# Convolution, Fourier mixing and a two-layer network on one core: copies moved to ScalarE, one more buffer for residuals and for normalised rows, two gathers placed earlier

## The chip, the core and the metric

The kernel runs on one core of a Trainium2 chip. The time is that of one launch on the device, in microseconds (us), taken here as the median of three runs. A core has five engines that work side by side, each through its own instructions in order: TensorE (PE in the profile, its weight loads PEld), VectorE (DVE), ScalarE (ACT), GpSimd (POOL) and SyncE (SP), which here only issues transfers. An engine that waits for a result holds back everything behind the waiting instruction in its own list, and nothing else.

## What is computed

```python
# x: (8, 4224, 192) f32; weight: (8, 7); w1: (192, 768); w2: (768, 192)
w = softmax(weight)                      # 7 taps for each of 8 heads of 24 columns
x = causal_conv(x, w)                    # along the sequence, each head its own taps
X = np.fft.fft(x, axis=1)
X = np.fft.fft(X, axis=2)
u = x + np.real(X)
un = (u - mean(u)) / np.sqrt(var(u) + 1e-06)
out = u + np.maximum(un @ w1, 0.0) @ w2
```

## The kernel before

The eight batches go through one program, each in two parts. The **front** of a batch makes its Fourier transform: the convolution in six chunks of three parts (conv_unit: products pc on TensorE at line 387, copied to xa on ScalarE or VectorE, stored to a scratch in DRAM, sc), its reload in another order (load_x, tile xs), a split of each value into two halves of 16 bits (split_x: XH on ScalarE at line 472, XL on VectorE at line 473), and two stages of products with tables (stage_a: pa, yh, yl; stage_b: pb). stage_b is called eight times a batch. Each call writes a tile V in two halves, one by ScalarE (line 524) and one by VectorE (line 525), and then copies the columns with q = 0, 128x96 values, from V to V0 (line 531). V0 collects these columns of all eight calls and is read only by the ninth step of the batch.

The **steps** are the rest: nine a batch, eight of 4 x 128 rows (it = 0 to 7) and one of 128 rows (it = 8). A step consists of
- load_res: the convolved rows xr, read back from sc by one indirect transfer per 128 rows, which GpSimd issues (line 544): four a step, one for it = 8. The tile xr has three buffers.
- prep: the last products pq (line 574), u copied from them by ScalarE in three pieces (line 591), xr added by GpSimd (line 592), mean and variance mv on VectorE (lines 598 and 599), then 1/sqrt: sd on ScalarE (line 610), w and nm on GpSimd (lines 611, 612), y on VectorE (line 613), and five small steps on GpSimd (lines 614 to 618), which refine y and leave nm = -mean * y. Then un = y * u + nm on ScalarE, four pieces (line 628; for steps 0 and 1 of batch 0 on VectorE, line 623), its upper 16-bit half into hl by ScalarE (line 638) and the rest into hl by GpSimd (line 641). The tile un has one buffer.
- transposes: kt from hl by a transposing transfer, which SyncE issues (line 651).
- mlp_hidden, six times: ph = kt @ w1 on TensorE (line 680), hh = max(ph, 0) in 16 bits on ScalarE (line 684), the remainder hlo on VectorE (line 685). ph has two buffers.
- mlp_out, four times: po = hh @ w2 on TensorE (lines 699, 702, 705), added to u on VectorE (line 711), and the store of u (SyncE).

In the main loop the hidden products of step n, the outputs of step n-1, the end of prep of step n+2 with its transposes, the first part of prep of step n+3 and the gathers of step n+4 are written interleaved; the front of later batches is spread over the steps by tables. A scheduler then takes this order as a wish and sets each engine's own list from it, from the tiles that are free and from its estimate of when each operand is there. So a change in buffers or in one operation's engine moves others too.

Ahead of the main loop stands a hand-written start for batch 0: the gathers of steps 0 and 1, stage_b 0 and 1, both steps' prep and transposes at high priority, then, held back until the last remainder of hl of step 1 has been issued (issue_after(lower[0])), the gathers of steps 2 and 3, then the convolution of batch 1.

from_float64 unpacks the 64-bit weights at the start and borrows the tags kt, hl and un for its scratch; the number of buffers given there must agree with the one in prep.

Of the kernel before, what the change touches and what calls it, by code (L numbers as in the profile page):

```python
# [11 lines left out]
F32 = mybir.dt.float32  # L12
I32 = mybir.dt.int32
U32 = mybir.dt.uint32
AF = mybir.ActivationFunctionType
# [4 lines left out]
B, S, D, HID = 8, 4224, 192, 768  # L20
# [105 lines left out]
def kernel(  # L126
# [13 lines left out]
    nc = tc.nc  # L140
    PSUM = bass.MemoryType.PSUM
    cp = ctx.enter_context(tc.tile_pool(name="cp", bufs=1))
    sb = ctx.enter_context(tc.tile_pool(name="sb", bufs=2))
# [79 lines left out]
    def from_float64(dst, raw, rows, n, name):  # L223

        lo_w, hi_w = (raw[:rows, :, i].bitcast(U32) for i in range(2))

        def tmp(i):
            t = sb.tile([128, HID], F32, tag=("kt", "hl", "un")[i], name=f"cv{i}_{name}", bufs=(3, 2, 1)[i])
            return t[:rows, :n]

        bits, aux, rem = tmp(0), tmp(1), tmp(2)
        V = nc.vector
        SL, SR = ALU.logical_shift_left, ALU.logical_shift_right
        bi, ai, ri = bits.bitcast(U32), aux.bitcast(U32), rem.bitcast(U32)

        V.tensor_scalar(ai, hi_w, 30, 30, op0=SR, op1=SL)
        V.tensor_scalar(bi, hi_w, 5, 2, op0=SL, op1=SR)
        V.tensor_tensor(bi, bi, ai, op=ALU.bitwise_or)
        V.scalar_tensor_tensor(bi, lo_w, 29, bi, op0=SR, op1=ALU.bitwise_or)

        V.tensor_scalar(ri, lo_w, 3, 3, op0=SL, op1=SR)
        V.tensor_scalar(ai, bi, 23, 23, op0=SR, op1=SL)
        V.scalar_tensor_tensor(rem, ri, 2.0 ** -52, aux, op0=ALU.mult, op1=ALU.mult)
        V.tensor_tensor(bits, bits, rem, op=ALU.add)

        V.tensor_scalar(ai, hi_w, 1, 21, op0=SL, op1=SR)
        V.scalar_tensor_tensor(dst, ai, 897, bits, op0=ALU.is_ge, op1=ALU.mult)
# [75 lines left out]
    def load_windows(bt, ch, tag="xt", bufs=2):  # L323

        b = bt.b
        n = D if b < NB0 else HP * GRP
        src = xw[b] if b < NB0 else xv[b - NB0]
        xt = sb.tile([WP, WC, D], F32, tag=tag, name=f"xt_{b}_{ch}", bufs=bufs)[:, :, :n]
        with tc.issue_after(turn[0]) if turn[0] else ExitStack():
            nc.sync.dma_start(xt, src[:, ch * WC : (ch + 1) * WC])  # L330
        bt.xt[ch] = xt
# [172 lines left out]
    def stage_b(bt, it):  # L504

        b = bt.b
        V = sb.tile([128, 2, 2 * NM, CG], F16, tag="V", name=f"V_{b}_{it}", bufs=5)
        for h in range(CG // CT):
            pb = ps.tile([128, CT, 2 * NM], F32, tag="f", name=f"pb_{b}_{it}_{h}", bufs=4)
            for i in range(CT):  # L510
                c = it * CG + h * CT + i

                parts = ((0, 2, NM),) if c else ((0, 1, NM), (1, 2, 0))
                for e0, e1, at in parts:
                    for n, (y, l) in enumerate(((bt.yh, 0), (bt.yh, 1), (bt.yl, 0))):
                        nc.tensor.matmul(
                            pb[NJ * e0 : NJ * e1, i],
                            y[:NBD, c, e0:e1].rearrange("p e j -> p (e j)"),
                            R[:, l, at : at + 2 * NM],
                            start=(n == 0), stop=(n == 2),  # L520
                        )
            src = pb.rearrange("p c m -> p m c")
            vh, vl = (V[:, l, :, h * CT : (h + 1) * CT] for l in range(2))
            nc.scalar.activation(vh, src, AF.Copy, scale=ESC)
            nc.vector.scalar_tensor_tensor(
                vl, src, ESC, vh, op0=ALU.mult, op1=ALU.subtract
            )

        if it == 0:
            bt.V0 = sb.tile([128, 2, 6, 64], F16, tag="V0", name=f"V0_{b}")  # L530
        nc.gpsimd.tensor_copy(
            bt.V0.rearrange("p l m c -> p (l m) c")[:, :, it * CG : (it + 1) * CG],
            V.rearrange("p l (m q) c -> p (l m) q c", q=NQ)[:, :, 0],
        )
        bt.V[it] = V


    def load_res(bt, it, g):

        b = bt.b  # L540
        if g == 0:
            bt.xr[it] = sb.tile([128, 4, D], F32, tag="xr", name=f"xr_{b}_{it}", bufs=3)
        col = 0 if it == Q0 else 1 + 4 * it + g
        nc.gpsimd.indirect_dma_start(  # L544
            bt.xr[it][:, g], None, bt.sc[:S],
            bass.IndirectOffsetOnAxis(ap=rows_sb[:, col : col + 1], axis=0),
        )

    def prep(bt, it):
        b = bt.b  # L550
        xr = bt.xr.pop(it)
# [54 lines left out]
        t = sb.tile([128, 4], F32, tag="t", name=f"t_{b}_{it}", bufs=3)[:, :ng]  # L606
# [10 lines left out]
        G_.tensor_tensor(y, y, t, op=ALU.mult)  # L617
        G_.tensor_tensor(nm, nm, y, op=ALU.mult)  # L618
        yield
        un = sb.tile([128, 4, D], F32, tag="un", name=f"un_{b}_{it}", bufs=1)  # L620
        for g in range(ng):
            if b == 0 and it < 2:
                nc.vector.tensor_scalar(
# [11 lines left out]
        hl = sb.tile([128, 3 * ng, 128], F16, tag="hl", name=f"hl_{b}_{it}")  # L635
# [11 lines left out]
    def transposes(bt, it):  # L647
        hl = bt.hl[it]
        n = hl.shape[1]
        kt = sb.tile([128, n, 128], F16, tag="kt", name=f"kt_{bt.b}_{it}", bufs=3)  # L650
        turn[0] = nc.sync.dma_start_transpose(kt, hl.rearrange("p n d -> p (n d)")).ins
        bt.kt[it] = kt.rearrange("p (g i) t -> p i g t", i=3)
# [93 lines left out]
    def call(f, *a):  # L746
        return lambda: f(*a)
# [43 lines left out]
    turn, lower = [None], [None]  # L791
    first = batches[0]
    for ch in range(NCH):
        tag, bufs = (("hlo", 2), ("xt", 2), ("yh", 1), ("yl", 1))[(0, 0, 1, 1, 2, 3)[ch]]
# [39 lines left out]
    def prep_piece(k):  # L834
        bt, it = steps[k]
        if k not in preps:
            preps[k] = prep(bt, it)
        next(preps[k])
# [4 lines left out]
    def gathers(k):  # L843
        bt, it = steps[k]
        return [call(load_res, bt, it, g) for g in range(1 if it == Q0 else 4)]
# [12 lines left out]
    with tc.issue_after(last_load):  # L858
        nc.sync.dma_start(rows_sb, rows)
        for ch in range(4):  # L860
            load_windows(batches[1], ch, *(("xt", 2), ("xs", 2))[ch // 2])
    for f in gathers(0) + gathers(1):
        f()
    stage_b(first, 0)
    stage_b(first, 1)

    for k in range(2):
        with tc.high_priority():
            for f in sums(k) + rest(k):
                f()  # L870
            transposes(first, k)
    with tc.issue_after(lower[0]):
        for f in gathers(2) + gathers(3):
            f()
    for ch in range(4):
        for part in range(3):
            conv_unit(batches[1], ch, part)
        if ch < 2:
            load_windows(batches[1], ch + 4)
    stage_b(first, 2)  # L880
    for f in sums(2):
        f()
    stage_b(first, 3)
    stage_b(first, 4)
    for n in range(len(steps) + 1):
        bt, it = steps[n] if n < len(steps) else (None, 0)
# [93 lines left out]
```

## Time and profile before

| | |
|---|---|
| time, median of 3 runs | 1337.24 us (1334.99, 1337.24, 1337.45) |
| the profiled execution: time, span | 1339.74 us, 1338.0 us |
| granted TensorE clock, mean | 0.96 of full |
| POOL L544, the gathers | 264, 283.0 us, 1072 ns each |
| POOL L531, the copies to V0 | 64, 17.9 us, 281 ns each |
| ACT L628, un | 256 pieces, 120.2 us, 539 ns each |
| steady period of a batch | 155.2 to 155.4 us |

The profile is of one execution. A row of a timeline gives the start, the time taken, the engine, the line, the operation, what it writes and reads, how many neighbours were joined (x), and in brackets how long the engine stood idle just before and what ended that. A group's row gives the sum and the mean of all instructions of a line. A row of windows gives the length of the stretch, each engine's busy time in it, the granted clock and the share of the transfer engines.

### The profile page before, as it was taken

The page shows a single profiled execution, that of the slowest core. Times are in us where ns is not written, and L with a number is a line of the kernel's source. Part 1 is how long each engine was busy: PE and PEld are TensorE (multiplying, and loading weights), DVE is VectorE, ACT ScalarE, POOL GpSimd, SP SyncE. Part 2 cuts the span into 40 slices and gives each one's busy share as a digit, 9 for nine tenths or more (in the row PEclk, how much of TensorE's full clock was granted, in tenths as well). Part 3 has the DMA queues.
Part 4 walks back from the last instruction along what each step waited for, and adds up shares of the span by engine and source line. Part 5 has one row for each costly group of instructions (what it writes and reads, how often), then busy time and mean ns, then how long its engine had stood idle before and what let it go on. Part 6 is the DMA issues. An engine that isn't in the chain of part 4 may idle for free.

```text
span 1338.0 us, 30108 instructions
## 1 busy us (share of the span) xinstructions
PE 1204.8 (90%) x12224; PEld 943.1 (70%) x12224; DVE 745.0 (56%) x1635; ACT 819.0 (61%) x1562; POOL 666.5 (50%) x1052
## 2 busy tenths in 40 slices
PE   4186689998999989998999989999889998999999
PEld 4175458885777767786778857777567876777767
DVE  7763365456545565456644575446654566555443
ACT  4643387558755686557865586556755667545642
POOL 0236535457445664457444574456634576456520
PEclk9588889998999999999999999999899999999999
DMA  8934395556555566456554576555564444223321
GB/s 274 241 90 125 90 246 142 104 132 166 132 124 128 126 149 144 121 129 167 120 139 103 122 178 127 128 125 129 141 137 108 116 96 95 69 63 84 75 63 39
DMA packets 225819, 170.19 MB, mean 127 GB/s; under 512 B 119560, under 2 KB 207440, under 8 KB 225680
## 3 DMA queue, kind: packets, MB, share of 16 engines
q1 hardware_dynamic: 163408, 108.53, 35.4%
q10 hardware_dynamic: 49600, 33.77, 10.0%
q0 software_dynamic: 12672, 25.97, 7.5%
q8 instruction: 95, 1.56, 0.5%
q14 instruction: 44, 0.36, 0.1%
HBM read 83.73 MB, written 58.55 MB: 106 GB/s over the span
## 4 chain that ended last, share of the span: by engine, by line
PE 35%; POOL 24%; issue 17%; ACT 11%; DVE 5%; DMA 4%; another core or an unknown queue 1%; SPq 1%; ACTq 0%; POOLq 0%; DVEq 0%
PE ph L680 12%; POOL xr L544 11%; PE pa L490 5%; ACT un L628 4%; POOL u L592 4%; PE po L699 4%; PE po L705 4%; PE po L702 4%; POOL hl L641 4%; DMA xs<-sc 3%; PE pc L387 3%; DVE XL L473 2%; PE pq L574 2%; ACT hl L638 2%; ACT hh L684 1%
## 5 line engine op out<-in xcount | busy, mean ns | idle before, releaser
L680 PE MATMUL ph<-kt,W 128*128 128x512 f16 (+1 forms) x2160 | 504.0, 367 | 18.5 <-DMA kt<-hl 8.4
L685 DVE SCALAR_TENSOR_TENSOR hlo<-ph,hh 128x512 f16<-128x512 f32 (+1 forms) x400 | 270.8, 679 | 346.5 <-ACT hh L684 342.0
L699 PE MATMUL po<-W,hh 128*128 128x192 f16 x1584 | 387.9, 248 | 45.7 <-ACT hh L684 34.1
L702 PE MATMUL po<-W,hh 128*128 128x192 f16 x1584 | 387.9, 248 | 1.3 <-issue 1.3
L705 PE MATMUL po<-W,hlo 128*128 128x192 f16 x1584 | 384.1, 247 | 1.8 <-issue 1.5
L684 ACT ACTIVATE hh<-ph 128x512 f16<-128x512 f32 (+1 forms) x400 | 236.5, 593 | 199.2 <-PE ph L680 141.3
L544 POOL DMA_INDIRECT xr<-sc,rows_sb x264 | 283.0, 1072 | 134.4 <-issue 60.7
L680 PEld LDWEIGHTS <-W 128*128 128x128 f16 x2160 | 196.4, 99 | 170.7 <-issue 25.7
L641 POOL TENSOR_TENSOR hl<-un,hl 128x512 f16<-128x512 f32 (+1 forms) x144 | 129.4, 920 | 219.0 <-ACT hl L638 210.4
L699 PEld LDWEIGHTS <-hh 128*128 128x128 f16 x1584 | 155.8, 98 | 58.9 <-ACT hh L684 38.6
L592 POOL TENSOR_TENSOR u<-u,xr 128x768 f32<-128x768 f32 (+1 forms) x72 | 121.1, 1682 | 129.9 <-ACT u L591 129.7
L702 PEld LDWEIGHTS <-hh 128*128 128x128 f16 x1584 | 155.8, 98 | 28.7 <-issue 14.1
L705 PEld LDWEIGHTS <-hlo 128*128 128x128 f16 x1584 | 155.6, 98 | 27.5 <-issue 5.8
L628 ACT ACTIVATE un<-u,nm,y 128x192 f32<-128x192 f32 x256 | 120.2, 539 | 53.9 <-POOL nm L618 49.5
L387 PE MATMUL pc<-xt,band 128*120 128x144 f32 x756 | 120.5, 301 | 24.2 <-DMA band<-line_d 15.0
L387 PEld LDWEIGHTS pc<-xt,band 128*120 128x120 f32 x756 | 107.3, 193 | 32.6 <-issue 16.1
L490 PE MATMUL pa<-c_sb,XH 128*128 128x128 f16 x1024 | 103.2, 223 | 22.2 <-ACT XH L472 19.1
L711 DVE SCALAR_TENSOR_TENSOR u<-po,fo,u 128x384 f32<-128x384 f32 (+1 forms) x136 | 81.4, 599 | 62.1 <-PE po L705 46.7
L473 DVE SCALAR_TENSOR_TENSOR XL<-xs,s_x,XH 128x768 f16<-128x768 f32 x64 | 104.2, 1638 | 17.1 <-ACT XH L472 10.3
L499 DVE SCALAR_TENSOR_TENSOR yl<-pa,yh 99x512 f16<-99x512 f32 x128 | 85.3, 682 | 49.1 <-ACT yh L498 45.7
L472 ACT ACTIVATE XH<-xs,s_x 128x768 f16<-128x768 f32 x64 | 106.3, 1694 | 7.9 <-DMA xs<-sc 7.9
L490 PEld LDWEIGHTS <-XH 128*128 128x128 f16 x1024 | 82.6, 99 | 32.6 <-ACT XH L472 19.7
(125 smaller groups left out, 1461.5 us busy)
## 6 DMA issues: line engine op xcount, KB each, us to landing
out_dram<-u SPq DMA_DIRECT2D x64, 384.0 KB
xt<-in_xw_dram SPq DMA_DIRECT2D x42, 576.0 KB
sc<-xa ACTq DMA_DIRECT2D x42, 540.0 KB
xs<-sc SPq DMA_DIRECT2D x96, 192.0 KB
xs<-sc SPq DMA_DIRECT2D x32, 216.0 KB
xr<-sc,rows_sb POOLq DMA_INDIRECT x264
sc<-xa ACTq DMA_DIRECT2D x7, 450.0 KB
xt<-in_xv_dram SPq DMA_DIRECT2D x6, 504.0 KB
```

The source lines that it names most:

```text
L387: nc.tensor.matmul(pc[:WR, h - h0], band[:, h, :WR], xt[:, :, h * GRP : (h + 1) * GRP], start=True, stop=True,)
L490: nc.tensor.matmul(pa[:, i], x[:, at], F[:, l], start=(n == 0), stop=(n == 2))
L544: nc.gpsimd.indirect_dma_start(bt.xr[it][:, g], None, bt.sc[:S], bass.IndirectOffsetOnAxis(ap=rows_sb[:, col : col + 1], axis=0),)
L592: nc.gpsimd.tensor_tensor(u[:, :ng], u[:, :ng], xr[:, :ng], op=ALU.add)
L628: nc.scalar.activation(un[:, g], u[:, g], AF.Identity, bias=nm[:, g : g + 1], scale=y[:, g : g + 1],)
L641: lower[0] = nc.gpsimd.tensor_tensor(bl[:, :, o : o + n], un[:, :ng, f], hi[:, :, f], op=ALU.subtract).ins
L680: nc.tensor.matmul(ph[:, n], W1[:, w, ht * 128 : (ht + 1) * 128], kt[:, k], start=(i == 0), stop=(i == len(order) - 1),)
L684: anchor[0] = nc.scalar.activation(hh, ph, AF.Relu).ins
L685: nc.vector.scalar_tensor_tensor(hlo, ph, 0.0, hh, op0=ALU.max, op1=ALU.subtract)
L699: nc.tensor.matmul(po[:, g % 2], hh[:, ht, tk], W2[:, ht, 0], start=(ht == 0), stop=False)
L702: nc.tensor.matmul(po[:, g % 2], hh[:, ht, tk], W2[:, ht, 1], start=False, stop=False)
L705: nc.tensor.matmul(po[:, g % 2], hlo[:, ht, tk], W2[:, ht, 0], start=False, stop=(ht == 5),)
```

## The change

Three edits. The copies to V0 run on ScalarE as an activation with AF.Copy. The tile xr has four buffers, and the gathers of steps 2 and 3 stand with those of steps 0 and 1, no longer held back. The tile un has two buffers.

```diff
--- before
+++ after
         def tmp(i):
-            t = sb.tile([128, HID], F32, tag=("kt", "hl", "un")[i], name=f"cv{i}_{name}", bufs=(3, 2, 1)[i])
+            t = sb.tile([128, HID], F32, tag=("kt", "hl", "un")[i], name=f"cv{i}_{name}", bufs=(3, 2, 2)[i])
...
-        nc.gpsimd.tensor_copy(
+        nc.scalar.activation(
             bt.V0.rearrange("p l m c -> p (l m) c")[:, :, it * CG : (it + 1) * CG],
             V.rearrange("p l (m q) c -> p (l m) q c", q=NQ)[:, :, 0],
+            AF.Copy,
         )
...
-            bt.xr[it] = sb.tile([128, 4, D], F32, tag="xr", name=f"xr_{b}_{it}", bufs=3)
+            bt.xr[it] = sb.tile([128, 4, D], F32, tag="xr", name=f"xr_{b}_{it}", bufs=4)
...
-        un = sb.tile([128, 4, D], F32, tag="un", name=f"un_{b}_{it}", bufs=1)
+        un = sb.tile([128, 4, D], F32, tag="un", name=f"un_{b}_{it}", bufs=2)
...
-    for f in gathers(0) + gathers(1):
+    for f in gathers(0) + gathers(1) + gathers(2) + gathers(3):
         f()
...
-    with tc.issue_after(lower[0]):
-        for f in gathers(2) + gathers(3):
-            f()
```

The lines from 532 on stand one lower in the changed kernel, so that the gathers are L545 there, un L629, hh L685. In the lists below a tile's name ends with the step within its batch and a serial number: u_3_1193 is u of step 3; in hh_1_3662<-ph_1_1_3736 the hidden values of step 1 are made from the second of its six products.

GpSimd at the start of batch 0, before: from the addition of step 2 to its normalisation.

```order
L531 COPY V_0_692<-V_6_1133 128x12x8
L592 TENSOR_TENSOR u_2_967<-u_2_967,xr_2_844 128x768
L592 TENSOR_TENSOR u_3_1193<-u_3_1193,xr_3_849 128x768
L544 DMA xr_5_1391<-sc_126,rows_sb 128x192 x4
L544 DMA xr_6_1616<-sc_126,rows_sb 128x192 x4
L531 COPY V_0_692<-V_7_1355 128x12x8
L611 TENSOR_SCALAR w_2_1003<-mv_2_991 128x4
L612 TENSOR_SCALAR nm_2_1004<-mv_2_991 128x4
L592 TENSOR_TENSOR u_4_1404<-u_4_1404,xr_4_1177 128x768
L614 TENSOR_TENSOR t_2_1002<-y_2_1001 128x4
L611 TENSOR_SCALAR w_3_1299<-mv_3_1260 128x4
```

The same engine there after the change:

```order
L593 TENSOR_TENSOR u_2_967<-u_2_967,xr_2_658 128x768
L545 DMA xr_6_1616<-sc_126,rows_sb 128x192 x4
L642 TENSOR_TENSOR hl_0_789<-un_0_784,hl_0_789 128x4x128
L642 TENSOR_TENSOR hl_0_789<-un_0_784,hl_0_789 128x4x64
L642 TENSOR_TENSOR hl_1_848<-un_1_843,hl_1_848 128x4x128
L642 TENSOR_TENSOR hl_1_848<-un_1_843,hl_1_848 128x4x64
L612 TENSOR_SCALAR w_2_1003<-mv_2_991 128x4
L613 TENSOR_SCALAR nm_2_1004<-mv_2_991 128x4
L615 TENSOR_TENSOR t_2_1002<-y_2_1001 128x4
L616 TENSOR_TENSOR t_2_1002<-t_2_1002,w_2_1003 128x4
L617 TENSOR_SCALAR t_2_1002<-t_2_1002 128x4
L618 TENSOR_TENSOR y_2_1001<-y_2_1001,t_2_1002 128x4
```

Before, the gathers of steps 5 and 6 and a copy to V0 stood between step 2's u and its chain (w, nm, t); now the gather of step 6 and the hl of steps 0 and 1 stand there. The gathers of steps 4 and 5 stand further ahead, behind u of step 1.

GpSimd in batch 1, steps 3 and 4 (each later batch reads alike), before:

```order
L592 TENSOR_TENSOR u_4_3745<-u_4_3745,xr_4_3524 128x768
L531 COPY V_1_2540<-V_7_3696 128x12x8
L611 TENSOR_SCALAR w_3_3648<-mv_3_3612 128x4
L612 TENSOR_SCALAR nm_3_3649<-mv_3_3612 128x4
L614 TENSOR_TENSOR t_3_3647<-y_3_3646 128x4
L544 DMA xr_7_4252<-sc_854,rows_sb 128x192 x4
L615 TENSOR_TENSOR t_3_3647<-t_3_3647,w_3_3648 128x4
L611 TENSOR_SCALAR w_4_3900<-mv_4_3808 128x4
L612 TENSOR_SCALAR nm_4_3901<-mv_4_3808 128x4
L614 TENSOR_TENSOR t_4_3899<-y_4_3898 128x4
L616 TENSOR_SCALAR t_3_3647<-t_3_3647 128x4
```

After:

```order
L593 TENSOR_TENSOR u_4_3745<-u_4_3745,xr_4_3524 128x768
L612 TENSOR_SCALAR w_3_3648<-mv_3_3612 128x4
L613 TENSOR_SCALAR nm_3_3649<-mv_3_3612 128x4
L615 TENSOR_TENSOR t_3_3647<-y_3_3646 128x4
L545 DMA xr_8_4568<-sc_854,rows_sb 128x192
L616 TENSOR_TENSOR t_3_3647<-t_3_3647,w_3_3648 128x4
L612 TENSOR_SCALAR w_4_3900<-mv_4_3808 128x4
L613 TENSOR_SCALAR nm_4_3901<-mv_4_3808 128x4
L617 TENSOR_SCALAR t_3_3647<-t_3_3647 128x4
L618 TENSOR_TENSOR y_3_3646<-y_3_3646,t_3_3647 128x4
L619 TENSOR_TENSOR nm_3_3649<-nm_3_3649,y_3_3646 128x4
```

Behind the first small step of t of step 3 stood the four gathers of step 7; now one gather stands there, that of step 8, and those of step 7 are ahead of u of step 4. The copy to V0 is gone.

ScalarE at the same steps, before:

```order
L610 ACTIVATE sd_4_3897<-mv_4_3808,eps 128x4
L684 ACTIVATE hh_1_3662<-ph_1_1_3736 128x512
L472 ACTIVATE XH<-xs_1_3405,s_x_3160 128x64x12
L684 ACTIVATE hh_1_3662<-ph_1_2_3797 128x512
L472 ACTIVATE XH<-xs_2_3636,s_x_3160 128x64x12 x2
L628 ACTIVATE un_3_3672<-u_3_3567,nm_3_3649,y_3_3646 128x192 x4
L684 ACTIVATE hh_1_3662<-ph_1_3_3835 128x512
L343 ACTIVATE sq_0_3845,nrm_3844<-xt_0_3450 128x1152
L638 ACTIVATE hl_3_3728<-un_3_3672 128x4x192
L684 ACTIVATE hh_1_3662<-ph_1_4_3883 128x512
L591 ACTIVATE u_5_3974<-pq_5_3973,g_1276 128x2x192
L591 ACTIVATE u_5_3974<-pq_5_3973,g_1276 128x2x64
```

After:

```order
L611 ACTIVATE sd_4_3897<-mv_4_3808,eps 128x4
L629 ACTIVATE un_3_3672<-u_3_3567,nm_3_3649,y_3_3646 128x192 x4
L685 ACTIVATE hh_1_3662<-ph_1_1_3736 128x512
L472 ACTIVATE XH<-xs_1_3405,s_x_3160 128x64x12
L639 ACTIVATE hl_3_3728<-un_3_3672 128x4x192
L629 ACTIVATE un_4_3931<-u_4_3745,nm_4_3901,y_4_3898 128x192 x4
L685 ACTIVATE hh_1_3662<-ph_1_2_3797 128x512
L472 ACTIVATE XH<-xs_2_3636,s_x_3160 128x64x12 x2
L639 ACTIVATE hl_4_3957<-un_4_3931 128x4x192
L685 ACTIVATE hh_1_3662<-ph_1_3_3835 128x512
L343 ACTIVATE sq_0_3845,nrm_3844<-xt_0_3450 128x1152
L685 ACTIVATE hh_1_3662<-ph_1_4_3883 128x512
```

un of step 3 moved from behind three XH to the place behind sd of step 4, ahead of the hh of step 1, and un and hl of step 4 moved ahead of its hh as well.

## The prediction

> **What bounds the kernel now.** I read the page's busy shares first, then the table of windows over one batch, then the waits of the engine that is busiest.
>
> ```profile
> PE 1204.8 (90%) x12224; PEld 943.1 (70%) x12224; DVE 745.0 (56%) x1635; ACT 819.0 (61%) x1562; POOL 666.5 (50%) x1052
> L699 PE MATMUL po<-W,hh 128*128 128x192 f16 x1584 | 387.9, 248 | 45.7 <-ACT hh L684 34.1
> L628 ACT ACTIVATE un<-u,nm,y 128x192 f32<-128x192 f32 x256 | 120.2, 539 | 53.9 <-POOL nm L618 49.5
> core 0: us, PE busy (x) PEld busy (x) DVE busy (x) ACT busy (x) POOL busy (x), PEclk, DMA share, GB/s
> 100.00:255.50 155.50, 126.85 (x1219) 97.93 (x1217) 75.63 (x160) 90.00 (x168) 74.96 (x119) 0.90 0.64 147
> 410.92:566.13 155.21, 147.94 (x1532) 116.05 (x1531) 86.24 (x189) 102.64 (x197) 84.44 (x132) 0.99 0.58 134
> ```
>
> TensorE sets the time: 90% over the span, and 147.94 of 155.21 us (95%) in a middle batch, with 7.3 us of gaps. The first batch's stretch is looser: 126.85 of 155.5, so 28.7 us idle. A change that gives TensorE no less work can win only in those two places. Its largest named wait after the start is for hh from ScalarE (34.1 us over the run), and ScalarE itself waits 49.5 us at un for nm from GpSimd. The rows of TensorE's timeline where the start and a middle batch lose most:
>
> ```profile
> 105.01 2.32 PE L680 MATMUL ph<-kt,W 128*128 128x512 f16 x10 [0.30 <-DMA kt<-hl]
> 123.32 0.34 PE L699 MATMUL po<-W,hh 128*128 128x192 f16 x1 [7.15 <-ACT hh L684]
> 166.89 4.33 PE L680 MATMUL ph<-kt,W 128*128 128x512 f16 x10 [8.09 <-DMA kt<-hl]
> 176.93 3.39 PE L387 MATMUL pc<-xt,band 128*120 128x144 f32 x16 [4.13 <-DMA xt<-in_xw_dram]
> 190.69 1.24 PE L680 MATMUL ph<-kt,W 128*128 128x512 f16 x5 [1.08 <-DVE hlo L685]
> 478.87 0.24 PE L699 MATMUL po<-W,hh 128*128 128x192 f16 x1 [1.71 <-DVE u L711]
> 482.05 0.34 PE L699 MATMUL po<-W,hh 128*128 128x192 f16 x1 [2.28 <-ACT hh L684]
> ```
>
> 105.01 is the first hidden product of step 0, 166.89 that of step 2 (step 1's stands between). The last two rows are the two larger gaps of batch 2.
>
> **The start: why step 2 comes late, and what the change does to it.** GpSimd's timeline:
>
> ```profile
> 68.40 0.95 POOL L544 DMA_INDIRECT xr<-sc,rows_sb  x1 [0.31 <-issue]
> 81.23 0.26 POOL L531 COPY V<-V 128x96 f16<-128x96 f16 x1 [11.88 <-DVE V L525]
> 83.64 3.61 POOL L592 TENSOR_TENSOR u<-u,xr 128x768 f32<-128x768 f32 x2 [1.17 <-ACT u L591]
> 98.72 1.78 POOL L641 TENSOR_TENSOR hl<-un,hl 128x512 f16<-128x512 f32 x2 [2.73 <-ACT hl L638]
> 104.84 1.08 POOL L544 DMA_INDIRECT xr<-sc,rows_sb  x1
> 118.90 0.95 POOL L544 DMA_INDIRECT xr<-sc,rows_sb  x1 [0.31 <-issue]
> 123.68 1.81 POOL L592 TENSOR_TENSOR u<-u,xr 128x768 f32<-128x768 f32 x1
> 131.20 0.99 POOL L544 DMA_INDIRECT xr<-sc,rows_sb  x1
> 140.01 0.95 POOL L544 DMA_INDIRECT xr<-sc,rows_sb  x1 [0.30 <-issue]
> 143.97 0.26 POOL L531 COPY V<-V 128x96 f16<-128x96 f16 x1 [3.02 <-DVE V L525]
> 158.27 0.35 POOL L618 TENSOR_TENSOR nm<-nm,y 128x4 f32<-128x4 f32 x2
> 161.31 1.78 POOL L641 TENSOR_TENSOR hl<-un,hl 128x512 f16<-128x512 f32 x2 [2.27 <-ACT hl L638]
> 103.10 1.22 ACT L591 ACTIVATE u<-pq,g 128x384 f32<-128x384 f32 x3 [0.29 <-PE pq L574]
> ```
>
> Step 2's u is ready on ScalarE at 104.3, but GpSimd adds its residual only at 123.68, since twelve gathers stand ahead (104.84 to 119.85, so 1.25 each), and normalises it at 158.3, since eight more gathers, a V copy that waits 3.02 and the gathers of step 7 stand ahead again. Afterwards the gathers of steps 2 and 3 are issued behind those of steps 0 and 1, in GpSimd's idle 69.35 to 81.23 (8 x 1.25 = 10.0 fits the 11.9), and no V copy is left there. By the new order, with these durations: u of 0 and 1 end at 87.25; the gathers of 4 and 5 (8 x 1.25) at 97.3; fourteen small steps of about 0.25 us at 100.8; u of step 2 waits for ScalarE until 104.3 and ends at 106.1; the gather of 6 (4 x 1.25) at 111.1; hl of step 0 at 112.9, of step 1 at 114.7; the chain, un, hl of step 2 at about 121. From hl's end to ph took 166.89 - 163.09 = 3.8 us, so **step 0's ph stands at about 117 instead of 105, step 2's input at 125 instead of 166.9**.
>
> Terms, for TensorE. (a) The wait of 8.09 goes: +8.1. (b) Behind it ten products took 4.33 us, where five later took 1.24 (248 each): 1.85 lost there, gone with the wait: +1.9. (c) xt at 176.93 is issued on SyncE behind step 2's transpose, which no longer holds the queue; but TensorE's new order also asks for it some 25 us sooner. It lands after the loads of batch 1 whose stores end in the 130s either way. From 0 to 4.1 gained; I take 2. (d) Step 0 is 12 us later. About one and a half steps of stage B are drawn ahead of it, and TensorE idled in that stretch anyway (7.15 at 123.32, with small waits for issue before it). If the 7.15 is the same idleness, the delay costs about 2; if it comes back as well, 9. I take 2. **Sum 8.1 + 1.9 + 2 - 2 = 10 us gained**; bounds 3 (7.15 comes back) and 17 (all of xt, no loss at step 0, 3 us of issue waits).
>
> [...]
>
> **The middle batches: what moves on GpSimd and ScalarE.** Times of batch 2, steps 3 and 4:
>
> ```profile
> 469.33 0.19 POOL L614 TENSOR_TENSOR t<-y 128x4 f32<-128x4 f32 x1
> 469.68 1.08 POOL L544 DMA_INDIRECT xr<-sc,rows_sb  x1 [0.16 <-POOL t L614]
> 476.31 0.56 POOL L615 TENSOR_TENSOR t<-t,w 128x4 f32<-128x4 f32 x1
> 476.95 1.35 POOL L611 TENSOR_SCALAR w<-mv 128x4 f32<-128x4 f32 x1
> 479.58 0.19 POOL L617 TENSOR_TENSOR y<-y,t 128x4 f32<-128x4 f32 x1
> 470.36 0.28 ACT L610 ACTIVATE sd<-mv,eps 128x4 f32<-128x4 f32 x1
> 479.66 1.86 ACT L628 ACTIVATE un<-u,nm,y 128x192 f32<-128x192 f32 x4 [3.46 <-POOL nm L618]
> 483.05 0.83 ACT L638 ACTIVATE hl<-un 128x768 f16<-128x768 f32 x1
> 485.33 0.60 ACT L684 ACTIVATE hh<-ph 128x512 f16<-128x512 f32 x1
> 470.50 1.56 DVE L473 SCALAR_TENSOR_TENSOR XL<-xs,s_x,XH 128x768 f16<-128x768 f32 x1
> L531 POOL COPY V<-V 128x96 f16<-128x96 f16 x64 | 17.9, 281 | 94.6 <-DVE V L525 94.5
> L524 ACT ACTIVATE V<-pb 128x408 f16<-128x408 f32 x128 | 63.6, 514 | 63.8 <-PE pb L516 23.9 <-remote 20.2 <-PE ph L680 18.2
> L213 ACT ACTIVATE r_x<-r_x 128x1 f32<-128x1 f32 x8 | 1.6, 203 | 18.2 <-DVE r_x L212 16.8 <-issue 1.4
> ```
>
> Between t and its successor stood four gathers (469.68 to 476.3); one stands there now. So nm of step 3 is ready after 469.7 + one gather (1.25) + six small steps (0.2 each): about 472.2, and about 473.5 if VectorE's XL, which runs from 470.50, stretches them as it stretched w at 476.95 (1.35 us). But un of step 3 also moves: from behind three XH to directly behind sd (ends 470.64), so it now waits W = 1.5 to 2.9 us there, with five hh of step 1 queued behind it. Between 470.64 and the end of hh at 485.9 ScalarE had the 3.46 of waiting; now it has W, and un and hl of step 4 (1.86 + 0.83 = 2.7) that stood behind. The last hh of step 1 moves by W + 2.7 - 3.46 = W - 0.8, so +0.7 to +2.1 us. TensorE waits there for hh already (2.28 at 482.05), so some of it is on the path; its own order puts products of step 0 ahead meanwhile. Bounds per batch: -0.8 (W = 0) and +2.1; I take +0.7, the smaller end, as part of it is covered. It occurs in six batches: **+4 us**, bounds -5 and +13.
>
> [...]
>
> **The 64 copies on ScalarE.** No such copy stands in the trace on ScalarE. Bounds: 203 ns (L213, one column) and 514 ns (L524, 408 columns); on GpSimd it took 281. It has 96 columns, so nearer to the lower row: I take 0.3, or 19 us of busy time in all (13 to 33). ScalarE is busy 102.64 of 155.21, so 8 x 0.3 = 2.4 per batch fit; it hurts only where one stands ahead of an hh that TensorE waits for. Each also waits for VectorE's half of V, on GpSimd 94.5/64 = 1.5 us each, now with hh behind. I take 1 us on the path in all; bounds 0 and 13 (a seventh of the wait per batch, or all 33 us at 40% exposure). [...]
>
> **The second un buffer** takes away a wait that ScalarE hardly has (un waits for nm, 49.5 of 53.9); it costs nothing by itself, and its effect is the new place of un, priced above. **The fourth xr buffer** moves the same 264 gathers earlier; 0 outside the start.
>
> **Sum.** -10 + 4 + 1 = -5 us from the profiled execution's 1339.74, so 1334.7. The median of the three runs is 1337.24, 2.5 lower, so the forecast is **1332.2 us** as a median. Measured against no change, about 0.2% (2.7 us) can be told.
>
> **The rivals.** *More is won* (0.2): the early nm does on ScalarE what the 49.5 us of waiting promises, and of TensorE's 34.1 - 7.15 = 27 us of waiting for hh half goes: -10 - 13 = -23, so 1314. For it: the gathers leave the middle of every chain. Against: un now waits at the front of ScalarE's queue. *ScalarE's queue* (0.25, the other side): un waits W = 2.9 with hh of step 1 behind it in six batches, +13, and the copies cost 5 rather than 1: -10 + 13 + 5 = +8, so 1345. It decides from the point where a batch loses 1.5 us (six times that eats nine of the ten won). For it: XL's stretch; against: TensorE's cover. *The start does not shorten* (0.15): step 0 at 117 costs all its 9, xt is waited for, so 3 won: -3 + 4 + 1 = +2, so 1339; the early gathers would only have exchanged which step is late. *Forecast* (0.4): 1326 to 1338.
>
> **Range.** From 1314 to 1346: the lower end is the larger gain, the upper that of ScalarE's queue; outside is left a start that both fails and pays. Faster by over 0.2% (below 1334.5): all of the first rival, 0.65 of the forecast's 0.4, 0.02 of the others: 0.48. Within 0.2%: 0.12 of the forecast's, 0.08 of the unshortened start's: 0.2. Slower: 0.32.
>
> **What would show it.** Right at the start: TensorE's first ph of step 0 near 117, that of step 2 near 150 without a wait for kt, and the stretch 100 to 255 busier than 126.85. In the middle: batch periods of 155.2 to 157.5, un of step 3 with a wait of 1.5 to 2.9 at sd. The copy: 0.27 to 0.35 us in ScalarE's group of line 531. I would be wrong if periods fall below 154 (un no longer blocks hh), or if step 2's ph still comes after 160.

## The result and the profile after

The changed kernel takes 1353.53 us (median of four runs, 1352.34 to 1355.44) where the kernel before, timed beside it, takes 1337.35: a ratio of 1.0124, with a 95% interval of 1.0108 to 1.0140. It is slower by 16 us. The forecast was 1332.2. The times and ratios below are of fast runs; the one slow run, of the kernel with the fourth xr buffer (1884.21 us at a granted clock of 0.612), is left out.

The changed kernel's page, the busy times and the rows that answer to those of before (lines stand one lower from 532 on):

```profile
PE 1208.6 (89%) x12224; PEld 941.0 (70%) x12224; DVE 747.0 (55%) x1635; ACT 830.7 (61%) x1626; POOL 644.2 (48%) x988
L700 PE MATMUL po<-W,hh 128*128 128x192 f16 x1584 | 386.9, 248 | 46.7 <-ACT hh L685 41.3
L629 ACT ACTIVATE un<-u,nm,y 128x192 f32<-128x192 f32 x256 | 119.9, 537 | 72.9 <-POOL nm L619 72.5
L531 ACT ACTIVATE V<-V 128x96 f16<-128x96 f16 x64 | 17.9, 280 | 18.3 <-DVE V L525 18.2
```

TensorE does the same work (1208.6 against 1204.8) in a longer span. Its wait for hh rose from 34.1 to 41.3 us although the 7.1 us of the start's largest one went out of it, and ScalarE's wait at un for nm rose from 49.5 to 72.5. The copies took what they took on GpSimd, 280 ns.

Where the 16 us arise is seen by laying both traces side by side at one instruction, the first hh of a step:

| first hh of | before, us | after, us | difference |
|---|---|---|---|
| batch 0, step 0 | 106.3 | 133.6 | +27.3 |
| batch 0, step 2 | 169.5 | 173.6 | +4.0 |
| batch 0, step 3 | 192.0 | 191.8 | -0.2 |
| batch 1, step 1 | 312.9 | 312.6 | -0.3 |
| batch 2, step 1 | 468.3 | 471.7 | +3.3 |
| batch 4, step 1 | 779.0 | 787.6 | +8.6 |
| batch 6, step 1 | 1094.4 | 1107.2 | +12.8 |
| batch 7, step 7 | 1316.7 | 1332.2 | +15.5 |

So the start came out even, where 10 us were forecast as won, and each middle batch loses about 3 us, in its steps 1 to 3: from the first hh of step 1 to that of step 4 it takes 59.9 us instead of 56.7 (mean of batches 1 to 4). Two things have to be explained.

**The start.** TensorE's timeline of the changed kernel, the waits from the first stage A to the first ph of step 0:

```profile
68.03 0.28 PE L490 MATMUL pa<-c_sb,XH 128*128 128x128 f16 x2 [0.79 <-issue]
75.04 0.27 PE L490 MATMUL pa<-c_sb,XL 128*128 128x128 f16 x1 [1.13 <-issue]
81.46 0.26 PE L490 MATMUL pa<-c_sb,XH 128*128 128x128 f16 x1 [1.16 <-issue]
105.16 1.81 PE L387 MATMUL pc<-xt,band 128*120 128x144 f32 x10 [3.11 <-issue]
131.22 4.42 PE L681 MATMUL ph<-kt,W 128*128 128x512 f16 x10 [8.76 <-DMA kt<-hl]
```

The products of stage A, which before ran back to back, come one or two at a time from 71.6 on, with gaps that no operand explains (13 waits of pa for issue, 9.2 us in all, against one of 0.3 in the kernel before). They lie where the gathers of steps 2 and 3 now run. The table of windows shows the same stretch, 69 to 81 us, first in the kernel before:

```profile
69.00:81.00 12.00, 10.59 (x184) 9.79 (x181) 9.88 (x16) 8.86 (x17) 0.35 (x1) 1.00 0.05 13
```

and in the changed kernel:

```profile
69.00:81.00 12.00, 4.14 (x31) 2.29 (x31) 2.21 (x4) 1.57 (x3) 7.61 (x9) 0.63 0.28 74
```

The columns are TensorE, its weight loads, VectorE, ScalarE, GpSimd, the granted clock, the share of the transfer engines, GB/s. 31 products are issued instead of 184, while the transfer engines are 28% busy, and VectorE and ScalarE stand idle most of the time too. The first V of batch 0 comes at 90.9 instead of 79.6 us.

**The middle.** ScalarE's timeline of the changed kernel in batch 2, steps 3 and 4, and under it GpSimd's, with one row of VectorE's, and TensorE's:

```profile
473.71 0.30 ACT L611 ACTIVATE sd<-mv,eps 128x4 f32<-128x4 f32 x1
477.08 1.86 ACT L629 ACTIVATE un<-u,nm,y 128x192 f32<-128x192 f32 x4 [3.07 <-POOL nm L619]
478.85 0.57 ACT L685 ACTIVATE hh<-ph 128x512 f16<-128x512 f32 x1
481.57 1.85 ACT L629 ACTIVATE un<-u,nm,y 128x192 f32<-128x192 f32 x4
490.66 1.21 ACT L592 ACTIVATE u<-pq,g 128x384 f32<-128x384 f32 x3 [0.89 <-DMA out_dram<-u]
491.75 0.60 ACT L685 ACTIVATE hh<-ph 128x512 f16<-128x512 f32 x1
```

```profile
473.15 1.06 POOL L545 DMA_INDIRECT xr<-sc,rows_sb  x1 [0.16 <-POOL t L615]
474.24 1.48 POOL L616 TENSOR_TENSOR t<-t,w 128x4 f32<-128x4 f32 x1
474.17 1.54 DVE L473 SCALAR_TENSOR_TENSOR XL<-xs,s_x,XH 128x768 f16<-128x768 f32 x1
476.85 0.20 POOL L619 TENSOR_TENSOR nm<-nm,y 128x4 f32<-128x4 f32 x1
```

```profile
479.48 0.26 PE L700 MATMUL po<-W,hh 128*128 128x192 f16 x1 [2.12 <-ACT hh L685]
483.10 0.24 PE L700 MATMUL po<-W,hh 128*128 128x192 f16 x1 [1.41 <-DVE u L712]
488.20 0.34 PE L700 MATMUL po<-W,hh 128*128 128x192 f16 x1 [1.27 <-ACT hh L685]
```

un of step 3 waits 3.07 us directly behind sd, five hh of step 1 stand behind it, and un of step 4 behind the first of these. One gather stands in nm's chain instead of four, yet the first small step behind it took 1.48 us where such a step takes 0.2, beside VectorE's XL of 1.54. In batches 1, 3, 4 and 5 the same step, at 315.17, 632.36, 790.13 and 948.64, took 1.47 or 1.48, each time beside an XL. TensorE waits for hh at 479.48 and 488.20. The last line of the first fence is the sixth hh of step 1, 20.1 us behind the first (471.65); in the kernel before that distance is 17.0.

### The profile page after: what moved, and what is told of

Its sections match the earlier page's. It is cut to its first block, busy times and chain, and to the rows that moved or that the text cites. A ratio compares the mean times of both kernels' runs of the same rounds, so it can differ in the third digit from the quotient of the medians.

```text
span 1353.5 us, 30076 instructions
## 1 busy us (share of the span) xinstructions
PE 1208.6 (89%) x12224; PEld 941.0 (70%) x12224; DVE 747.0 (55%) x1635; ACT 830.7 (61%) x1626; POOL 644.2 (48%) x988
## 4 chain that ended last, share of the span: by engine, by line
PE 44%; POOL 15%; ACT 12%; issue 12%; DVE 9%; DMA 5%; SPq 1%; POOLq 0%; ACTq 0%; another core or an unknown queue 0%; DVEq 0%
PE ph L681 17%; POOL xr L545 7%; PE po L700 5%; PE po L706 5%; PE po L703 5%; PE pa L490 5%; ACT un L629 4%; DVE XL L473 4%; PE pc L387 3%; POOL u L593 3%; PE pq L575 3%; DMA out_dram<-u 3%; ACT XH L472 2%; POOL hl L642 2%; DVE hlo L686 2%
## 5 line engine op out<-in xcount | busy, mean ns | idle before, releaser
L700 PE MATMUL po<-W,hh 128*128 128x192 f16 x1584 | 386.9, 248 | 46.7 <-ACT hh L685 41.3
L685 ACT ACTIVATE hh<-ph 128x512 f16<-128x512 f32 (+1 forms) x400 | 235.0, 589 | 197.1 <-PE ph L681 149.6
L545 POOL DMA_INDIRECT xr<-sc,rows_sb x264 | 280.3, 1062 | 134.7 <-issue 60.7
L629 ACT ACTIVATE un<-u,nm,y 128x192 f32<-128x192 f32 x256 | 119.9, 537 | 72.9 <-POOL nm L619 72.5
L387 PE MATMUL pc<-xt,band 128*120 128x144 f32 x756 | 116.6, 296 | 20.1 <-DMA band<-line_d 15.0
L490 PE MATMUL pa<-c_sb,XH 128*128 128x128 f16 x1024 | 106.0, 225 | 25.3 <-ACT XH L472 18.4
L387 PEld LDWEIGHTS pc<-xt,band 128*120 128x120 f32 x756 | 104.2, 189 | 28.9 <-issue 18.3
L498 ACT ACTIVATE yh<-pa 99x512 f16<-99x512 f32 x128 | 74.6, 598 | 62.0 <-PE pa L490 24.9
L472 ACT ACTIVATE XH<-xs,s_x 128x768 f16<-128x768 f32 x64 | 105.8, 1684 | 10.4 <-DMA xs<-sc 6.7
## 6 DMA issues: line engine op xcount, KB each, us to landing
xs<-sc SPq DMA_DIRECT2D x96, 192.0 KB
```

The costliest lines, as they stand in the source:

```text
L387: nc.tensor.matmul(pc[:WR, h - h0], band[:, h, :WR], xt[:, :, h * GRP : (h + 1) * GRP], start=True, stop=True,)
L490: nc.tensor.matmul(pa[:, i], x[:, at], F[:, l], start=(n == 0), stop=(n == 2))
L545: nc.gpsimd.indirect_dma_start(bt.xr[it][:, g], None, bt.sc[:S], bass.IndirectOffsetOnAxis(ap=rows_sb[:, col : col + 1], axis=0),)
L629: nc.scalar.activation(un[:, g], u[:, g], AF.Identity, bias=nm[:, g : g + 1], scale=y[:, g : g + 1],)
L685: anchor[0] = nc.scalar.activation(hh, ph, AF.Relu).ins
L700: nc.tensor.matmul(po[:, g % 2], hh[:, ht, tk], W2[:, ht, 0], start=(ht == 0), stop=False)
```

## The experiments

The runs were spread over several chips, and the kernel before takes 1336 to 1338 us on some of them and 1314 on two. Each ratio is to the kernel before on the same chip. "Period" is a quarter of the time from the first hh of step 1 in batch 1 to that in batch 5; "six hh" the time from the first to the sixth hh of step 1 in batch 2; W the wait of un of step 3 there.

| run | ratio (95%) | period | six hh | W | first V |
|---|---|---|---|---|---|
| before, again | 1 (single run) | 155.1 | 17.0 | 3.46 | 79.4 |
| changed kernel, again | 1.0116 (1.0101 to 1.0132) | 158.6 | 20.1 | 3.08 | 92.2 |
| without the second un buffer | 1.0095 (1.0078 to 1.0112) | 157.9 | 18.0 | 3.06 | 91.3 |
| without the copies on ScalarE | 1.0011 (0.9997 to 1.0026) | 156.2 | 17.9 | 1.92 | 89.3 |
| un late, all three edits | 0.9847 (0.9834 to 0.9861) | 152.9 | 15.6 | 0 | 92.7 |
| gathers held, all three edits | single run, 1357.5 us | 158.6 | 20.2 | 3.08 | 79.0 |
| un late, copies, new start | 0.9791 (0.9778 to 0.9805) | 153.5 | 15.5 | 0 | 79.3 |
| *chips with 1314:* copies alone | 0.9992 (0.9978 to 1.0006) | 153.4 | 17.6 | 3.98 | 79.1 |
| second un buffer alone | 1.0138 (1.0120 to 1.0157) | 155.7 | 19.5 | 3.46 | 80.4 |
| fourth xr buffer alone | 1.0053 (1.0039 to 1.0066) | 154.9 | 18.1 | 1.91 | 81.1 |
| fourth xr buffer, early gathers | 1.0013 (1.0001 to 1.0025) | 155.3 | 18.1 | 1.91 | 79.7 |
| before, un late | 0.9807 (0.9789 to 0.9824) | 150.3 | 15.3 | 0 | 78.8 |

### One edit at a time

The copies alone:

```diff
-        nc.gpsimd.tensor_copy(
+        nc.scalar.activation(
...
+            AF.Copy,
```

> The copies to V0 on ScalarE alone; xr keeps three buffers, un one, the gathers of steps 2 and 3 stay held back. In this kernel un of step 3 stays behind the three XH on ScalarE. Theory A (the middle batches lose because un of steps 3 and 4 stands ahead of the hh of step 1 on ScalarE): nothing moves, 1335 to 1340 us, batch period 155.2 to 155.6. Theory B (the 64 copies themselves hold ScalarE up): the 16 us are here, 1350 or more, period about 157.9.

Ratio 0.9992: nothing. Theory B, that the copies by themselves hold ScalarE up, falls; ScalarE's list keeps un where it was.

The second un buffer alone:

```diff
-        un = sb.tile([128, 4, D], F32, tag="un", name=f"un_{b}_{it}", bufs=1)
+        un = sb.tile([128, 4, D], F32, tag="un", name=f"un_{b}_{it}", bufs=2)
```

> The second un buffer alone. On ScalarE un of step 4 now stands directly behind un of step 3, and un and hl of step 4 (2.7 us) ahead of the last hh of step 1. Theory A: the last hh of step 1 comes up to 2.7 us later, so period 156.5 to 158 and 1345 to 1354 us. Theory B: 1337, period 155.2.

Ratio 1.0138: on this chip one line loses as much as the whole change did. ScalarE's timeline of this kernel in batch 2:

```profile
467.54 3.61 ACT L628 ACTIVATE un<-u,nm,y 128x192 f32<-128x192 f32 x8 [3.46 <-POOL nm L618]
471.05 0.57 ACT L684 ACTIVATE hh<-ph 128x512 f16<-128x512 f32 x1
473.89 0.83 ACT L638 ACTIVATE hl<-un 128x768 f16<-128x768 f32 x1
```

Eight pieces of un in one go, steps 3 and 4 together, with the hh behind them, and step 4's hl among them. The sixth hh comes 19.5 us behind the first, 1.9 later than in the copies alone on the same chip (17.6); 2.7 was worked out from un and hl of step 4. With one buffer, un of step 4 could not start before the hl of step 3 had read the buffer; that had kept it out of the way.

The fourth xr buffer alone, and with the early gathers:

```diff
-            bt.xr[it] = sb.tile([128, 4, D], F32, tag="xr", name=f"xr_{b}_{it}", bufs=3)
+            bt.xr[it] = sb.tile([128, 4, D], F32, tag="xr", name=f"xr_{b}_{it}", bufs=4)
```

> The fourth xr buffer alone, gathers of steps 2 and 3 still held back. On ScalarE un of step 3 stands behind one hh and one XH of step 1 rather than directly behind sd, un of step 4 ahead of the last hh, its hl behind it. Theory A: the last hh moves by 1.86 plus the wait of un for nm minus 3.46; with a wait of 1 to 3 that is -0.6 to +1.4 a batch, so 1333 to 1346. Theory B: 1337. The start gains only from the order behind the held gathers, 0 to 5 us.

> Fourth xr buffer and the early gathers, copies on GpSimd, un with one buffer. The middle as in the run with the fourth buffer alone. The start tells whether the sixteen gathers in a row slow TensorE: theory C (gaps of issue in the first stage A come with the gathers that run beside it): the first V of batch 0 at 90 to 92 us as in the changed kernel, instead of 80. Rival D (the gaps have to do with the copies on ScalarE or the un buffer): the first V at 80 to 81.

1.0053 and 1.0013. The periods (154.9, 155.3) lie 1.5 and 1.9 above the 153.4 of the copies alone, which stand for the kernel before on that chip. The sum W + 1.86 - 3.46 gives +0.3 for the hh, and they moved by 0.6 against the copies alone; so the rest of the 1.5 is lost elsewhere, and the sum doesn't cover it. The early gathers give back some 5 us at the start (1320.8 to 1315.8). And on this chip stage A is not disturbed, with the same sixteen gathers in a row:

```profile
69.00:81.00 12.00, 10.37 (x184) 9.77 (x183) 9.79 (x16) 9.42 (x19) 8.36 (x9) 1.00 0.30 83
```

The gaps of theory C stay out, as rival D expected. But the kernel lacks the copies and the un buffer and the chip is another too, and the next runs speak for the chip.

### The whole change again, and without one edit

> The changed kernel as it is, on the chip on which the single edits were timed. Theory A (un and hl of step 4 ahead of the last hh of step 1 cost a middle batch 2.5 us): the middle loses 15 us against before. Theory C (sixteen gathers in a row starve TensorE's issue): first V of batch 0 near 91 us as in the first profile; if that is a matter of the chip or the moment (rival D2), it stands near 80 here and the start gains 5 to 10, so that the ratio is 1.004 to 1.010 rather than 1.012.

> The kernel before as it is, for its profile on this chip. Without the gaps of issue behind the gathers of steps 2 to 4 (theory D2) the first hh of step 2 comes near 152 us instead of 169.5; with them it is near 169 again.

These two ran on another chip than the single edits, one of those with 1337. The first V is at 92.2 and the gaps are back; the ratio is that of the first measurement. The kernel before loses time in the same manner where its own twelve gathers run (104.84 to 119.85): its wait of 7.15 at 123 in the prediction's rows is 8.70 here, and its step 2 has its first hh at 169.2. On the chips with 1314 it comes at 152 to 158 in the kernels that keep the start. The stretch of these twelve gathers as windows, first in the first profile of the kernel before, then in the copies alone on a chip with 1314:

```profile
104.00:124.00 20.00, 9.32 (x89) 5.70 (x87) 5.20 (x9) 5.46 (x12) 13.51 (x19) 0.81 0.49 141
104.00:124.00 20.00, 20.00 (x204) 15.51 (x202) 13.31 (x41) 12.03 (x26) 16.16 (x16) 1.00 0.68 193
```

That speaks for D2, that this belongs to the chip, and so do the two runs that follow on it: each leaves out one of the edits, and the gaps are there all the same (first V at 91.3 and 89.3). No kernel with the early gathers ran on both kinds of chip. The ratio that D2 expected was for a chip without the gaps.

> Copies on ScalarE, fourth xr buffer, early gathers; un with one buffer. On ScalarE un of step 3 stands directly behind sd of step 4 as in the whole change, three of the four pieces of un of step 4 ahead of the hh of the fourth product, the last piece and hl ahead of the last hh. Theory A: the middle loses 1.5 to 2.5 us a batch, ratio 1.007 to 1.012. Theory E (it is the second un buffer by itself): nothing, ratio 1.000 to 1.002.

> Second un buffer, fourth xr buffer, early gathers; the copies stay on GpSimd. On ScalarE un of steps 3 and 4 stand together behind one hh and one XH of step 1, ahead of its last four hh. Theory A: 1.5 to 2.5 us a batch, ratio 1.007 to 1.012. Theory F (the early nm lets un start sooner and pays for it): 0 to 1 us a batch, ratio 1.000 to 1.005.

Without the second un buffer the ratio is 1.0095: theory A's range, and E falls. Here un of step 3 stands directly behind sd again, with the wait of 3.06; the six hh lose only 1.0 of the 2.8 us of the period. 1.6 more are lost within step 2 (from its first hh to that of step 3 19.3 us instead of 17.6), where TensorE waits 1.00 for XL at 493.71. Without the copies on ScalarE, the other two edits kept, the ratio is 1.0011: un of step 3 then stands behind one hh and one XH, W is 1.9, and a batch loses 1.1. By the ratio that is F's range, not A's. So the cheap copies matter, though not by their time; the lists show how: with them and the fourth xr buffer un goes up directly behind sd.

### The place of un alone

All three edits stay; the end of prep is asked for behind the fourth product of the step rather than behind the first, and un is held behind the hh just written:

```diff
-                nc.scalar.activation(
-                    un[:, g], u[:, g], AF.Identity,
+                with in_turn():
+                    nc.scalar.activation(
+                        un[:, g], u[:, g], AF.Identity,
...
-            place(rest(n + 2), 0, 1)
-            place([call(transposes, *steps[n + 2])], 3, 1)
+            place(rest(n + 2), 6, 1)
+            place([call(transposes, *steps[n + 2])], 8, 1)
```

> All three edits as in the changed kernel; only un moves: the end of prep is asked for four products later, and un is held on ScalarE behind the hh of the product just written, so that un of step 3 stands behind the fourth hh of step 1 (as in the kernel before), with nm long ready, and no un of step 4 stands among the hh of step 1. Theory A (the middle batches lose by the place of un and its wait): the middle loses nothing or wins, from hh of the first to hh of the sixth product of step 1 at most 17 us instead of 20.1, period 153 to 155.3, ratio to the kernel before 0.985 to 1.002. Rival G (three edits take the time elsewhere, by buffers, copies or transfers): period stays near 158, ratio 1.010 or more.

Ratio 0.9847, where the same three edits without it give 1.0124, and the disturbed start is kept (first V at 92.7). ScalarE's timeline in batch 2, the fourth hh of step 1 and un of step 3:

```profile
471.13 0.57 ACT L686 ACTIVATE hh<-ph 128x512 f16<-128x512 f32 x1
471.61 1.85 ACT L630 ACTIVATE un<-u,nm,y 128x192 f32<-128x192 f32 x4
473.37 1.61 ACT L472 ACTIVATE XH<-xs,s_x 128x768 f16<-128x768 f32 x1
```

un waits for nothing any more, and one un stands among the hh of a step. TensorE's waits in this kernel:

```profile
PE po L701 <- ACT hh L686: 10.2, 13, 1.6
```

41.3 us became 10.2. From the first hh of step 1 to that of step 4 a batch takes 56.6 us again (56.7 before, 59.9 in the changed kernel): what the middle had lost is back. Another 2.2 us a batch are won around step 0: from its first hh to that of step 1 16.0 us instead of 20.8, less 2.6 lost in the steps from 4 on. Rival G falls: the buffers, copies and transfers are all still there. And the last version below, on the same chip and without the two buffers, has a period of 153.5 beside 152.9 here, so once un is late the buffers cost the middle nothing.

The same in the kernel before, with nothing else changed:

> The kernel before with nothing but un placed late, as in the run of the whole change with un late; copies on GpSimd, three xr buffers, one un buffer, start as before. Theory A: the middle wins as there, period 153 to 154, 8 to 14 us in all, ratio 0.988 to 0.995, and the three edits add nothing to that in the middle. If the gain there needed the early nm, which the fourth xr buffer brings: 0.997 to 1.003.

Ratio 0.9807, below the expected range: the gain was there to be had without any of the three edits, and it doesn't need the early nm. It isn't won in step 1, as theory A would have it: from the first hh of step 1 to that of step 4 a batch takes 57.0 us, and 56.1 in the copies alone on such a chip. It is won from the first hh of step 0 to that of step 1, 16.2 us instead of 20.7. There un of step 2 now stands behind the sixth hh instead of behind the first, and products pc of a convolution have left that stretch as well; what each is worth is not separated.

### The gathers at the start

The changed kernel with the gathers of steps 2 and 3 behind u of step 1:

```diff
-    for f in gathers(0) + gathers(1) + gathers(2) + gathers(3):
+    for f in gathers(0) + gathers(1):
         f()
...
+    with tc.issue_after(adds[1]):
+        for f in gathers(2) + gathers(3):
+            f()
```

> The changed kernel, but the gathers of steps 2 and 3 held on GpSimd behind the addition of step 1's residual, thus behind the first stage A. Theory C (gathers in a row slow TensorE's issue, where the chip shows it at all): the first V of batch 0 at 80 us, no gaps of issue in stage A; the gaps come with the gathers, now between 87 and 112 us. Rival: the gaps stay in stage A at 68 to 82 us whatever GpSimd does, first V near 91. Middle as in the changed kernel, period 158.

Windows of this kernel, stage A and then the stretch of the gathers:

```profile
69.00:81.00 12.00, 10.45 (x180) 9.69 (x180) 10.01 (x18) 8.86 (x17) 0.00 (x0) 1.00 0.04 11
88.00:108.00 20.00, 5.78 (x46) 4.88 (x44) 4.94 (x17) 0.81 (x2) 15.48 (x21) 0.65 0.61 184
```

TensorE's largest gap in it:

```profile
104.37 0.33 PE L516 MATMUL pb<-c_sb,yh 99*128 99x102 f16 x2 [8.34 <-issue]
```

Stage A is whole, the first V at 79.0, and the gaps moved with the gathers: 46 products in 20 us, another stage and other operands. On this chip a row of gathers slows what TensorE issues. The end is much the same as with the early gathers (1357.5 in a single run; the changed kernel's runs lie between 1350 and 1357), since the gaps only changed place.

A version from this: the kernel before with the copies on ScalarE, un late, and at the start step 4's gathers behind step 2's u and those of steps 5 and 6 behind the normalisation of steps 2 and 3.

```diff
+        after = None
+        if b == 0 and it > 3:
+            after = adds.get(2) if it == 4 else nms.get(it - 3)
+        with tc.issue_after(after) if after is not None else ExitStack():
```

> The kernel before with the copies on ScalarE, un placed late as in the run before, and at the start the gathers of step 4 behind the addition of step 2, those of steps 5 and 6 behind the normalisation of steps 2 and 3; three xr buffers, one un buffer. Theory A: period 153 to 155, so 0 to 13 us won in the middle; at the start step 2's input comes 10 to 25 us sooner where the gathers slowed TensorE, 0 to 10 us won. Ratio 0.982 to 0.998. If neither counts: 1.000.

Ratio 0.9791, below both kernels, and below 0.982, where the range ended. Step 2's first hh comes at 145.7 instead of 169.2. How much of the gain is the start's is not separated: un late in the kernel before gave 0.9807 on a chip without the gaps, and the two intervals overlap.

## Why the prediction was wrong

The sum was -10 for the start, +4 for the middle, +1 for the copies. Measured: 0, about +16, 0.

- **Start, the step that failed:** "in GpSimd's idle 69.35 to 81.23 (8 x 1.25 = 10.0 fits the 11.9)". They did fit, from 69.35 to 79.05, but that GpSimd was idle did not make them free: TensorE's stage A was stretched, and the first V came 11.4 us later. The delays behind were followed rightly: ph of step 0 was put at 117 and came at 131.2, which is 117 and 11, with 3 more because u of step 2 left ScalarE at 118.3, 14 behind the 104.3 used. The wait of 8.09 at step 2 went, as term (a) said, and so did that for xt, term (c). But an idle time of the same size (8.76) stood ahead of step 0 in its place, with ten slow products behind it (4.42 us, 442 ns each, where five at 474.31 took 248), so (a) and (b) came back there, where term (d) had put 2. Term (d) was too small without the gaps too: with the fourth xr buffer and the early gathers, on a chip with 1314, step 0's ph came at 112.5 behind an idle time of 5.57, and the early gathers won 5 us, not 10. The rows that could have warned were read otherwise: TensorE's idle time at 113 to 123 in the kernel before was taken as there anyway; it lies beside that kernel's own twelve gathers.
- **Middle, the term that was mis-sized:** the mechanism was right, in the place that was named, but +0.7 a batch was taken from -0.8 to +2.1, and 3.0 was measured (158.3 against 155.3). W came at 3.07, over the upper end of 2.9: the step beside XL took 1.48, where 1.35 had been read. (The XL shown in the prediction ends at 472.06; the 1.35 lies beside later ones, 475.30 to 478.29.) W - 0.8 then gives +2.3; the six hh moved by 3.1, of which 0.89 is a new wait of u of step 5 for the store of its buffer. The reason given for the lower end, that TensorE's products of step 0 cover part, did not hold: the period rose by as much as the six hh moved, and TensorE's idle time per batch from 7.1 to 9.3 us.
- **The copies:** 280 ns and no measurable cost by themselves; 0.3 and 1 were taken. What they change in ScalarE's list was not in the sum: leaving them out of the whole change takes its ratio from 1.0116 to 1.0011.
- **The second un buffer:** "it costs nothing by itself" is wrong: alone it costs 1.4%, by the place that it lets un of step 4 take. That the wait of un for its buffer was short (4 us in all) was taken to mean that the buffer did not matter; it mattered by the order that it forced. Within the whole change it is worth less: leaving it out gives 1.0095 instead of 1.0116.
- **The rivals:** the one of ScalarE's queue (0.25, 1345) has the middle nearly right, with +13; the one in which the start doesn't shorten (0.15) has the start, though in part by another cause. They were priced one without the other. By their own terms together (-3, +13, and +5 for the copies) they give 1352, near the 1353.53, and that is luck in part: the start won nothing, and the copies took nothing by themselves.

What remains open: why the gathers slow TensorE's issue on some chips and not on others, what of a gather does it, why step 2 loses time as well in the kernel without the second un buffer, and what the gain around step 0 with un late is made of.

## What to carry to other kernels

An added buffer is also a change of order: look where the instructions that it sets free go in an in-order engine's list, and who stands behind them; here one more buffer cost 1.4%, and asking for the end of prep three products later, with un held behind an hh, won 1.9% with no new resource (which part of that is un's place alone is not separated). An operation that waits belongs behind those that feed the bottleneck engine, not ahead of them, even if its own operand gets earlier. An idle stretch of one engine is not free for its transfers until a row shows the bottleneck engine at full rate beside such transfers.

## What the runs showed of the hardware

On the chips with 1337, long rows of indirect gathers (0.95 us at the median, one every 1.25) went along with gaps in what TensorE issues: in the row of the changed kernel from the eleventh gather on (71.85; three gaps of 0.79 us stand ahead of it), with TensorE's busy time in 12 us down from 10.6 to 4.1 and the transfer engines at 28%. The eight at the start of the kernel before (56.99 to 69.35; TensorE busy 7.02 of the 7.71 us from its first product at 61.64 on) and the four in a row of its middle batches (27 such rows from 450 to 1000 us, TensorE busy 140.8 of their 146.3 us) went without such gaps; how many it takes is not shown. On a chip with 1314 a row of sixteen left it at 10.4, with the transfer engines at 30%. And one and the same kernel takes 1314 us on some chips and 1337 on others, 1.8% apart, where its own runs on one of them lie within 0.5% of their median, so only ratios taken on one chip could be compared.
